# Pooled attention and token/channel mixer on one core: cast DMAs in long rows, pooling by GpSimd adds, shared batch tails and a hand-woven TensorE order

## The chip, the core and the metric

The kernel runs on one core of one Trainium2 chip. The metric is the device time of one execution in microseconds (us). The engines are TensorE (PE; its weight loads are shown as PEld), VectorE (DVE), ScalarE (ACT), GpSimd (POOL) and SyncE (SP); 16 DMA engines move data between the device memory and the on-chip buffer. TensorE writes only into PSUM, eight banks of 2 KB per partition, from which VectorE or ScalarE carries results away.

## The reference

For each of 8 batches: attention of 8 heads with 576 tokens and head size 64, whose keys and values are first averaged over groups of 8 tokens (72 pooled tokens), and then a mixer with a token layer (576 to 256 to 576) and a channel layer (512 to 1536 to 512).

```python
k_p = k.reshape(B, H, 72, 8, 64).mean(axis=3)
v_p = v.reshape(B, H, 72, 8, 64).mean(axis=3)
scores = scale * (q @ k_p.transpose(0, 1, 3, 2))
attn = exp(scores - max) / (sum + 1e-09)
x = (attn @ v_p).transpose(0, 2, 1, 3).reshape(B, 576, 512)
h = relu(x.transpose(0, 2, 1) @ w_tok1) @ w_tok2
u = x + h.transpose(0, 2, 1)
out = u + relu(u @ w_ch1) @ w_ch2
```

## The kernel before

576 tokens are four blocks of 128 and one of 64 (`csize`). All matmuls are in bf16. `load_qkv` copies q, k and v of a batch by 15 DMAs from the GpSimd queue that also convert float32 to bf16; each takes one block of tokens and its rows in the device memory are 64 floats (256 bytes) long. Weights come by SyncE's queue in float32 and are cast by ScalarE and VectorE.

Stage A of a batch pools k and v on TensorE: ten matmuls of 512 columns with the averaging matrix `p_full` (L118, L120). It then transposes the pooled keys (L131) and q (L141), and makes scores per head with a contraction over 64 rows, in a piece of 512 columns and one of 64 (L153, L155); ScalarE takes their exponents (L157, L158). `mk_av` multiplies by the pooled values with a column of ones beside them (L169), so that VectorE can divide by the sum (L173, L175). Stage B is the token layer (L189, L203) with transposes of `u` (L208). Stage C is the channel layer: per block of 128 hidden channels four matmuls of 512 columns and four of 64 (L226, L229), evacuated by ScalarE and VectorE in turn, and then for each of the five token blocks twelve matmuls of 512 columns (L246), whose sum VectorE adds to `u` (L249) and ScalarE's queue writes out.

Five batches are in flight: iteration `it` works on stage A of batch `it`, its `mk_av` steps one iteration later, stage B two, stage C three and four later. `weave` spreads the steps of those lists evenly over each other, and a scheduler then orders the instructions of every engine; 12 iterations run. PSUM has four one-bank buffers `pa`, two of `pb` and two of `pt`.

Of the kernel before, what the change touches and what calls it, by code (L numbers as in the profile page):

```python
# [26 lines left out]
):  # L27
    nc = tc.nc
    B, H, S, D = q.shape
    P = 128  # L30
    NC = 5
    TAIL = S - 4 * P
    POOL = 8
    SP = S // POOL
    DM = H * D
    DT = moe_w_tok1.shape[1]
    DC = moe_w_ch1.shape[1]
    scale = 1.0 / (D ** 0.5)
# [25 lines left out]

    w_tok1_sb = singles.tile([P, NC, DT], BF16)
    w_tok2_sb = singles.tile([P, 2, S], BF16)
    w_ch1_sb = singles.tile([P, 4, DC], BF16)
    w_ch2_sb = singles.tile([P, 12, DM], BF16)

    with tc.tile_pool(name="wtmp", bufs=1) as wtmp:  # L70
        wf1 = wtmp.tile([P, NC, DT], FP32, name="wf")
        nc.sync.dma_start(out=wf1[:, 0:4, :], in_=moe_w_tok1[0:4 * P, :].rearrange("(c p) n -> p c n", p=P))
        nc.sync.dma_start(out=wf1[0:TAIL, 4, :], in_=moe_w_tok1[4 * P:S, :])
        nc.gpsimd.memset(w_tok1_sb[:, 4, :], 0.0)
        nc.vector.tensor_copy(out=w_tok1_sb[:, 0:4, :], in_=wf1[:, 0:4, :])
        nc.vector.tensor_copy(out=w_tok1_sb[0:TAIL, 4, :], in_=wf1[0:TAIL, 4, :])

        wf2 = wtmp.tile([P, 2, S], FP32, name="wf")
        nc.sync.dma_start(out=wf2, in_=moe_w_tok2.rearrange("(c p) n -> p c n", p=P))
        nc.vector.tensor_copy(out=w_tok2_sb, in_=wf2)  # L80

        wf3 = wtmp.tile([P, 4, DC], FP32, name="wf")
        nc.sync.dma_start(out=wf3, in_=moe_w_ch1.rearrange("(c p) n -> p c n", p=P))
        nc.scalar.copy(out=w_ch1_sb[:, 0:2, :], in_=wf3[:, 0:2, :])
        nc.vector.tensor_copy(out=w_ch1_sb[:, 2:4, :], in_=wf3[:, 2:4, :])

        wf4 = wtmp.tile([P, 12, DM], FP32, name="wf")
        nc.sync.dma_start(out=wf4, in_=moe_w_ch2.rearrange("(c p) n -> p c n", p=P))
# [166 lines left out]
    def weave(lists):  # L255
# [83 lines left out]
```

## Time and profile before

| | |
|---|---|
| three runs | 382.47, 383.92 (median) and 386.97 us |
| the profiled execution, first to last instruction (its span) | 382.7 us |
| its end: last matmul group L246 from 365.58 to 378.66 us, last L249 at 378.68 us | some 4 us behind the last matmul |
| TensorE matmuls | 339.0 us busy, 89%, 2320 |
| VectorE, ScalarE, GpSimd | 164.0 (43%), 122.4 (32%), 106.2 us (28%) |
| bytes read from and written to the device memory | 35.78 and 9.44 MB |

The profile lists no separate device time for the execution that it shows; its span lies within the three runs and 1.2 us under their median. Matmuls overlap in the pipeline, so that the duration of one (380 ns for 512 columns) is longer than the distance to the next (some 217 ns), and a busy TensorE is not one at its peak. The pace of TensorE is therefore read from the starts of successive matmuls.

### The profile page before, as it was taken

Reading aid. Unit: us, or ns where it says so; the run is one execution under the profiler, and the core shown is the slowest. Engines: PE = TensorE matmul, PEld = TensorE weight load, DVE = VectorE, ACT = ScalarE, POOL = GpSimd, SP = SyncE. Lnnn points to the kernel's source line nnn. Section 1 sums busy time; section 2 is a strip of 40 time slices with the busy share of each in tenths; the row PEclk is TensorE's granted clock in tenths of the full one; section 3 lists DMA queues with packets and bytes.
Section 4 is the critical chain, followed back from the end, with each engine's and each line's share of the span. In section 5 each row is a group of like instructions: output and inputs, shape, how many; then the busy total and the mean of one; then the engine's idle time right before and its main releaser. Section 6 shows DMA issues by size and latency. Waiting matters only on the chain.

```text
span 382.7 us, 5680 instructions
## 1 busy us (share of the span) xinstructions
PE 339.0 (89%) x2320; PEld 158.9 (42%) x2320; DVE 164.0 (43%) x389; ACT 122.4 (32%) x299; POOL 106.2 (28%) x138
## 2 busy tenths in 40 slices
PE   0305657999999999999999999999999999999995
PEld 0002233445544444444445444444444544444442
DVE  1003025665664455354454554445545544443332
ACT  1005519465633353244323451335312212112100
POOL 9819469889717300813000000000000000000000
PEclk9999999999999999999999999999999999999999
DMA  9999999999939471989000100001100101111122
GB/s 146 211 299 120 314 158 124 148 102 140 118 22 143 56 71 41 82 98 93 27 15 27 57 27 15 27 29 42 29 29 28 57 14 57 38 32 55 55 70 69
DMA packets 120745, 31.43 MB, mean 82 GB/s; under 512 B 113232, under 2 KB 113808, under 8 KB 120720
## 3 DMA queue, kind: packets, MB, share of 16 engines
q0 software_dynamic: 112512, 14.16, 60.4%
q10 hardware_dynamic: 5248, 9.44, 7.2%
q1 hardware_dynamic: 2960, 7.47, 5.6%
q8 instruction: 18, 0.29, 0.3%
q14 instruction: 7, 0.06, 0.1%
HBM read 35.78 MB, written 9.44 MB: 118 GB/s over the span
## 4 chain that ended last, share of the span: by engine, by line
PE 83%; DMA 8%; POOL 5%; ACT 2%; issue 0%; DVE 0%; POOLq 0%
PE pa L246 28%; PE pa L226 23%; PE pa L189 5%; PE pa L203 5%; PE pa L153 4%; DMA qb<-in_q_dram 4%; DMA vb<-in_v_dram 4%; PE pb L169 4%; PE pb L229 3%; PE pt L208 3%; PE pa L118 2%; PE pa L120 2%; PE pt L141 2%; POOL vb L100 2%; POOL qb L100 2%; POOL kb L100 2%
## 5 line engine op out<-in xcount | busy, mean ns | idle before, releaser
L246 PE MATMUL pa<-w_ch_sb,GT 128*128 128x512 bf16 (+1 forms) x480 | 112.3, 380 | 0.0
L226 PE MATMUL pa<-uT,w_ch_sb 128*128 128x512 bf16 x384 | 102.6, 380 | 0.0
L249 DVE TENSOR_TENSOR o<-pa,u 128x512 f32<-128x512 f32 (+1 forms) x40 | 27.6, 690 | 91.6 <-PE pa L246 91.6
L246 PEld LDWEIGHTS <-GT 128*128 128x128 bf16 (+1 forms) x480 | 44.9, 100 | 49.5 <-issue 3.6
L232 ACT ACTIVATE GT<-pa 128x512 bf16<-128x512 f32 x48 | 28.7, 597 | 82.4 <-PE pa L226 57.9
L157 ACT ACTIVATE expT<-pa 72x512 bf16<-72x512 f32 x64 | 37.3, 597 | 37.9 <-PE pb L155 35.2
L226 PEld LDWEIGHTS <-w_ch_sb 128*128 128x128 bf16 x384 | 31.2, 98 | 34.3 <-issue 10.8
L144 ACT COPY qT<-pt 128x512 bf16<-128x512 bf16 (+1 forms) x40 | 21.4, 546 | 74.4 <-PE pt L141 74.3
L100 POOL DMA_DIRECT2D qb<-in_q_dram x40 | 36.1, 912 | 28.9 <-PE pb L229 18.5
L118 PE MATMUL pa<-kb,p_full 128*72 128x512 bf16 (+1 forms) x40 | 18.4, 464 | 27.2 <-DMA kb<-in_k_dram 27.2
L235 DVE TENSOR_SCALAR GT<-pa 128x512 bf16<-128x512 f32 x48 | 33.1, 690 | 21.0 <-PE pa L226 20.5
L100 POOL DMA_DIRECT2D vb<-in_v_dram x40 | 37.4, 936 | 9.2 <-DMA qb<-in_q_dram 9.2
L100 POOL DMA_DIRECT2D kb<-in_k_dram x40 | 35.8, 896 | 6.2 <-PE pa L120 4.3
L175 DVE TENSOR_TENSOR x<-pb,den 128x256 bf16<-128x256 f32 (+1 forms) x80 | 32.8, 420 | 1.7
L205 DVE TENSOR_TENSOR u<-pa,x 128x512 bf16<-128x512 f32 (+1 forms) x40 | 27.2, 679 | 11.1 <-PE pa L203 11.0
L229 PEld LDWEIGHTS <-w_ch_sb 128*128 128x128 bf16 x384 | 23.3, 98 | 20.2 <-DVE x L175 0.6
L229 PE MATMUL pb<-uT,w_ch_sb 128*128 128x64 bf16 x384 | 26.4, 193 | 0.0
L169 PE MATMUL pb<-vp,expT 72*128 72x65 bf16 (+1 forms) x320 | 23.4, 201 | 2.3 <-ACT expT L158 2.2
L153 PE MATMUL pa<-qT,kpT 64*72 64x512 bf16 x64 | 24.3, 451 | 1.2 <-ACT qT L144 0.6
L122 DVE CAST kp<-pa 72x512 bf16<-72x512 f32 x8 | 5.5, 685 | 45.3 <-PE pa L118 45.3
L125 POOL MEMSET vp<- 72x8 bf16 x8 | 1.5, 191 | 83.9 <-issue 42.9
L203 PE MATMUL pa<-AT,w_tok_sb 128*128 128x512 bf16 (+1 forms) x80 | 24.5, 380 | 0.0
(44 smaller groups left out, 261.9 us busy)
## 6 DMA issues: line engine op xcount, KB each, us to landing
out_dram<-o ACTq DMA_DIRECT2D x32, 256.0 KB, 2.0
wf<-in_moe_w_ch_dram SPq DMA_DIRECT2D x2, 3072.0 KB, 14.4
qb<-in_q_dram POOLq DMA_DIRECT2D x32, 128.0 KB, 4.5
kb<-in_k_dram POOLq DMA_DIRECT2D x32, 128.0 KB, 4.9
vb<-in_v_dram POOLq DMA_DIRECT2D x32, 128.0 KB, 5.3
out_dram<-o ACTq DMA_DIRECT2D x8, 128.0 KB, 2.3
wf<-in_moe_w_tok_dram SPq DMA_DIRECT2D x1, 576.0 KB, 6.6
wf<-in_moe_w_tok_dram SPq DMA_DIRECT2D x1, 512.0 KB, 3.5
```

The lines of the kernel that those rows point to most:

```text
L100: nc.gpsimd.dma_start(out=dst[0:cs, c], in_=src_[b, :, c * P:c * P + cs, :].rearrange("h p d -> p h d"))
L153: nc.tensor.matmul(out=sc_ps, lhsT=kpT_sb[hl * D:(hl + 1) * D, pr, :], rhs=qT_sb[hl * D:(hl + 1) * D, pr, 0:512], start=True, stop=True)
L157: nc.scalar.activation(out=expT_sb[:, h, 0:512], in_=sc_ps, func=AF.Exp, scale=scale)
L169: nc.tensor.matmul(out=ao[half][0:cs, hh, :], lhsT=expT_sb[:, h, c * P:c * P + cs], rhs=vp_sb[:, h, :], start=True, stop=True)
L175: nc.vector.tensor_tensor(out=x_sb[0:cs, c, half * 4 * D:(half + 1) * 4 * D].rearrange("p (h d) -> p h d", d=D), in0=ao[half][0:cs, :, 0:D ...
L203: nc.tensor.matmul(out=u_ps[0:cs, :], lhsT=w_tok2_sb[:, m, c * P:c * P + cs], rhs=AT_sb[:, m, :], start=(m == 0), stop=(m == 1))
L226: nc.tensor.matmul(out=g_ps, lhsT=w_ch1_sb[:, kk, m * P:(m + 1) * P], rhs=uT_sb[:, kk, 0:512], start=(kk == 0), stop=(kk == 3))
L229: nc.tensor.matmul(out=g_ps2, lhsT=w_ch1_sb[:, kk, m * P:(m + 1) * P], rhs=uT_sb[:, kk, 512:S], start=(kk == 0), stop=(kk == 3))
L232: nc.scalar.activation(out=GT_sb[:, m, 0:512], in_=g_ps, func=AF.Relu)
L235: nc.vector.tensor_scalar(out=GT_sb[:, m, 0:512], in0=g_ps, scalar1=0.0, scalar2=None, op0=ALU.max)
L246: nc.tensor.matmul(out=o_ps[0:cs, :], lhsT=GT_sb[:, kk, c * P:c * P + cs], rhs=w_ch2_sb[:, kk, :], start=(kk == 0), stop=(kk == 11))
L249: nc.vector.tensor_tensor(out=o_sb[0:cs, :], in0=o_ps[0:cs, :], in1=u_sb[0:cs, c, :], op=ALU.add)
```

## The change

Nearly all of the kernel is written anew; the mathematics and the bf16 matmuls stay.

- Tokens are grouped by p = t // 9 and r = t % 9. With that, one partition reads 9 whole rows of q (2304 bytes), and one partition of k or v reads the 8 tokens of a pooled token (2048 bytes). A batch is loaded by three converting DMAs in place of 15 (batch 0 by six), and the weights by converting DMAs as well, all from the GpSimd queue but `w_tok2`, which comes by SyncE's queue and is cast on chip.
- k and v are pooled by additions (`pool8`): three per half tensor, on VectorE for batch 0, on GpSimd for the others. The pooled keys are written twice, side by side, and their transposes go into a 128-row buffer of which one half is zero, so that scores contract over 128 rows in pieces of 320 and 256 columns.
- The ninth block r (64 tokens) of two batches shares one 128-row tile `xt`; the tails of all eight batches make one more channel-layer unit of 512 tokens (n == B). A unit is then 48 matmuls L287 and 48 matmuls L300 of 512 columns, and there are nine units.
- The orders of TensorE and GpSimd are those of the code (`manual_schedule`); VectorE and ScalarE are still ordered by the scheduler. Unit n carries as its side the attention and token layer of batch n + 1, batch 0's stand alone ahead of unit 0. PSUM: three one-bank `p1`, two two-bank `p2`, one `pt`.

```diff
-    for src_, dst in ((q, qb), (k, kb), (v, vb)):
-        nc.gpsimd.dma_start(out=dst[0:cs, c],
-                            in_=src_[b, :, c * P:c * P + cs, :].rearrange("h p d -> p h d"))
+    def load(b):
...
+        parts = 2 if b == 0 else 1
+        def kv(t, src, g):
+            n = H // parts
+            nc.gpsimd.dma_start(out=t[:, g * n:(g + 1) * n].rearrange("j h i d -> j h (i d)"),
+                                in_=src[b, g * n:(g + 1) * n].rearrange("h (j i) d -> j h (i d)", i=POOL))
+        for g in range(parts):
+            kv(kr, k, g)
+            n = HP // parts
+            nc.gpsimd.dma_start(
+                out=qb[:, g * n * BR * D:(g + 1) * n * BR * D].rearrange("p (a e) -> p a e", a=n),
+                in_=q[b, 2 * g * n:2 * (g + 1) * n].rearrange("(a l) (p r) d -> (l p) a (r d)", l=2, r=BR))
+        for g in range(parts):
+            kv(vr, v, g)
...
+    def load_ch():
+        for g in range(3):
+            cols = slice(g * 512, (g + 1) * 512)
+            nc.gpsimd.dma_start(out=w_ch1[:, :, cols], in_=moe_w_ch1[:, cols].rearrange("(c p) n -> p c n", p=P))
+        for g in range(2):
+            nc.gpsimd.dma_start(out=w_ch2[:, 6 * g:6 * g + 6, :],
+                                in_=moe_w_ch2[g * 768:(g + 1) * 768, :].rearrange("(c p) n -> p c n", p=P))
+    def pool8(eng, t, hs, dst, dup):
+        n = hs.stop - hs.start
+        t4 = att.tile([SP, H // 2, 4, D], FP32, name="t4")
+        eng.tensor_tensor(out=t4[:, 0:n], in0=t[:, hs, 0:4], in1=t[:, hs, 4:8], op=ALU.add)
+        eng.tensor_tensor(out=t4[:, 0:n, 0:2], in0=t4[:, 0:n, 0:2], in1=t4[:, 0:n, 2:4], op=ALU.add)
+        if dup:
+            eng.tensor_tensor(out=dst, in0=t4[:, 0:n, 0, None, :].broadcast_to([SP, n, 2, D]),
+                              in1=t4[:, 0:n, 1, None, :].broadcast_to([SP, n, 2, D]), op=ALU.add)
+        else:
+            eng.tensor_tensor(out=dst, in0=t4[:, 0:n, 0], in1=t4[:, 0:n, 1], op=ALU.add)
...
+            eng = nc.vector if first else nc.gpsimd
...
+        def score(hp, odd):
+            n, c0 = (OD, EV) if odd else (EV, 0)
...
+                    nc.tensor.matmul(out=ps[0:SP, hl, 0:n], lhsT=kT[:, odd, h * SP:(h + 1) * SP],
+                                     rhs=st["qT"][:, hp, hl, 0:n], start=True, stop=True)
...
+                nc.scalar.activation(out=exv[:, 2 * hp:2 * hp + 2, c0:c0 + n], in_=ps[0:SP, :, 0:n],
+                                     func=AF.Exp, scale=scale)
...
+        steps += [av(c) for c in range(5)]
+        steps += [at(0), at(1), u(0), u(1), uT(0), u(2), uT(1), u(3)]
+        steps += ([u(4), uT(2), uT(4)] if par else [uT(2)]) + [uT(3)]
...
+        return [g(m) for m in range(NM)] + [o(c, part) for c in range(4) for part in range(3)]
...
+    with tc.manual_schedule(engines={PE, POOLE}):
+        load(0)
...
+        make_identity(nc, ident)
+        load_tok()
+        load_ch()
+        load(1)
+        batches = [batch_steps(b) for b in range(B)]
+        batches[0][0]()
+        for s in batches[0][1]:
+            s()
+        for n in range(B + 1):
+            main = unit_steps(n, batches[n][2] if n < B else None)
+            side = []
+            if n + 1 < B:
+                load(n + 2)
+                batches[n + 1][0]()
+                side = batches[n + 1][1]
+            lo, hi = (14, 26) if n == 0 else (0, 22)
+            at = [lo + i * (hi - lo) // max(1, len(side)) for i in range(len(side))]
+            for i in range(max(len(main), hi + 1)):
+                if i < len(main):
+                    main[i]()
+                for j, s in enumerate(side):
+                    if at[j] == i:
+                        s()
```

How the orders stand at three places. On TensorE before, in the middle of the program, a score of 64 contraction rows stands between groups of the channel layer and of `mk_av`:

```order
L246 MATMUL pa<-w_ch_sb,GT 128x512
L153 LDWEIGHTS kpT
L153 MATMUL pa<-qT,kpT 72x512
L155 LDWEIGHTS kpT
L155 MATMUL pb<-qT,kpT 72x64
L169 LDWEIGHTS expT
L169 MATMUL pb<-vp,expT 128x65
```

On TensorE now, at the start of unit 1 (`pt_769` takes the pooled keys of batch 2 and `pt_780` the first part of its q; both are the one buffer `pt`; rows that repeat are left out):

```order
L287 MATMUL p1_763<-uT_388,w_ch1_86 128x512
L176 LDWEIGHTS kp_734
L176 MATMUL pt_769<-ident_82,kp_734 128x72
...
L189 LDWEIGHTS qb_358
L189 MATMUL pt_780<-ident_82,qb_358 128x128
...
L287 LDWEIGHTS w_ch1_86
L287 MATMUL p1_787<-uT_388,w_ch1_86 128x512
```

The 64-row shapes are gone from such places; what stands between two uses of `pt` is at some places four channel matmuls, and here, between L176 and L189, nothing.

On GpSimd now, at the start of unit 1 (`kr_727` and its fellows are batch 3; `kr_356` is batch 2, whose keys TensorE wants from unit 1 on):

```order
L85 DMA kr_727<-in_k_dram 72x8x512
L90 DMA qb_729<-in_q_dram 128x4x576
L85 DMA vr_728<-in_v_dram 72x8x512
L153 MEMSET vp_735 72x8
L154 MEMSET ex_736 72x64
L130 TENSOR_TENSOR t4_739<-kr_356 72x1024
L131 TENSOR_TENSOR t4_739<-t4_739 72x4x128
L133 TENSOR_TENSOR kp_734<-t4_739 72x512
```

Before, that queue held only DMA issues and a small memset; now the pooling of a batch stands behind the issue of the next one's load, whose q has to wait until the buffer of the batch two before it has been transposed.

On VectorE now, for batch 0, the transposed keys are copied only behind the pooling of its values:

```order
L133 TENSOR_TENSOR kp<-t_149 72x512
L130 TENSOR_TENSOR t_153<-vr 72x1024
L130 TENSOR_TENSOR t_157<-vr 72x1024
L131 TENSOR_TENSOR t_153<-t_153 72x4x128
L131 TENSOR_TENSOR t_157<-t_157 72x4x128
L136 TENSOR_TENSOR vp<-t_153 72x4x64
L136 TENSOR_TENSOR vp<-t_157 72x4x64
L169 MEMSET xt 128x256 x2
L180 COPY kTs_91<-pt 64x288 x4
```

Before, VectorE's part ahead of the scores was three instructions (L122, L126, L133), with no load of its own to wait for.

## Rows read from the trace of the kernel before

**Rows 1.** The page: busy time, and PE and DMA in 40 slices of the span.
```profile
PE 339.0 (89%) x2320; PEld 158.9 (42%) x2320; DVE 164.0 (43%) x389; ACT 122.4 (32%) x299; POOL 106.2 (28%) x138
PE   0305657999999999999999999999999999999995
DMA  9999999999939471989000100001100101111122
```

**Rows 2.** Chain of waits in time: start, length (us), what.
```profile
10.90 15.74 DMA qb<-in_q_dram
...
38.71 15.09 DMA vb<-in_v_dram
...
85.71 0.97 PE pa L226 x4
...
157.31 1.18 PE pa L189 x5
...
198.48 1.18 PE pa L189 x5
...
239.65 1.18 PE pa L189 x5
...
365.58 13.08 PE pa L246 x60
378.68 0.68 DVE o L249
```

**Rows 3.** Timeline of PE, steady part: start, length (us), line, operation, out<-in, shapes, count.
```profile
202.19 0.39 PE L141 MATMUL pt<-ident,qb 128*128 128x128 bf16 x4
202.41 1.03 PE L226 MATMUL pa<-uT,w_ch_sb 128*128 128x512 bf16 x4
203.28 0.28 PE L229 MATMUL pb<-uT,w_ch_sb 128*128 128x64 bf16 x4
203.39 0.29 PE L169 MATMUL pb<-vp,expT 72*128 72x65 bf16 x4
203.53 0.39 PE L141 MATMUL pt<-ident,qb 128*128 128x128 bf16 x4
...
212.93 0.82 PE L246 MATMUL pa<-w_ch_sb,GT 128*128 128x512 bf16 x3
213.68 0.22 PE L155 MATMUL pb<-qT,kpT 64*72 64x64 bf16 x1
213.83 2.12 PE L246 MATMUL pa<-w_ch_sb,GT 128*128 128x512 bf16 x9
215.88 0.40 PE L153 MATMUL pa<-qT,kpT 64*72 64x512 bf16 x1
216.12 0.19 PE L155 MATMUL pb<-qT,kpT 64*72 64x64 bf16 x1
216.24 1.04 PE L226 MATMUL pa<-uT,w_ch_sb 128*128 128x512 bf16 x4
```

**Rows 4.** Groups by line and shape: busy us, mean ns of one, idle before.
```profile
L205 DVE TENSOR_TENSOR u<-pa,x 128x512 bf16<-128x512 f32 x32 | 21.9, 685 | 10.7 <-PE pa L203 10.6
L175 DVE TENSOR_TENSOR x<-pb,den 128x256 bf16<-128x256 f32 x64 | 26.4, 422 | 1.5
L173 DVE RECIPROCAL den<-pb 128x4 f32<-128x4 f32 x64 | 10.8, 176 | 21.1 <-PE pb L169 21.0
L213 DVE COPY uT<-pt 128x512 bf16<-128x512 bf16 x16 | 6.8, 423 | 7.6 <-PE pt L208 7.6
L133 DVE COPY kpT<-pt 128x288 bf16<-128x288 bf16 x8 | 2.4, 305 | 1.7 <-PE pt L131 1.7
L157 ACT ACTIVATE expT<-pa 72x512 bf16<-72x512 f32 x64 | 37.3, 597 | 37.9 <-PE pb L155 35.2 <-PE pa L153 2.3
```

**Rows 5.** Page: DMA queues, packets, MB, share of 16 engines' span (q0: GpSimd's, q1: SyncE's).
```profile
q0 software_dynamic: 112512, 14.16, 60.4%
q1 hardware_dynamic: 2960, 7.47, 5.6%
```

**Rows 6.** Timeline of all engines, start of the program.
```profile
0.81 0.41 SPq L72 DMA_DIRECT2D wf<-in_moe_w_tok_dram  x1
4.34 0.90 DVE L75 CAST w_tok_sb<-wf 128x1024 bf16<-128x1024 f32 x1 [4.34 <-DMA wf<-in_moe_w_tok_dram]
15.15 0.58 PE L120 MATMUL pa<-vb,p_full 128*72 128x512 bf16 x1 [0.38 <-DMA vb<-in_v_dram]
17.91 0.58 PE L120 MATMUL pa<-vb,p_full 128*72 128x512 bf16 x1 [0.34 <-DMA vb<-in_v_dram]
31.82 0.45 PE L131 MATMUL pt<-ident,kp 72*64 72x72 bf16 x8 [0.23 <-DVE kp L122]
32.54 1.75 DVE L85 CAST w_ch_sb<-wf 128x3072 bf16<-128x3072 f32 x1
32.57 2.21 POOL L100 DMA_DIRECT2D vb<-in_v_dram  x1
43.45 1.49 PE L120 MATMUL pa<-vb,p_full 128*72 128x512 bf16 x3
43.56 0.22 ACT L158 ACTIVATE expT<-pb 72x64 bf16<-72x64 f32 x1 [0.30 <-PE pb L155]
```

**Rows 7.** Groups by line and shape, POOL.
```profile
L100 POOL DMA_DIRECT2D qb<-in_q_dram x40 | 36.1, 912 | 28.9 <-PE pb L229 18.5 <-DMA kb<-in_k_dram 7.9 <-PE pa L153 2.4
L60 POOL TENSOR_SCALAR_AFFINE_SELECT p_full<-p_full 128x360 bf16<-128x360 bf16 x1 | 0.5, 505 | 0.0
L59 POOL MEMSET p_full<- 128x360 bf16 x1 | 0.4, 402 | 0.0
```

More of the change, by code (lines that the diff above doesn't have):

```diff
@@ L12 @@
 ALU = mybir.AluOpType
+PE = mybir.EngineType.PE
+POOLE = mybir.EngineType.Pool
 @with_exitstack
@@ L68 @@
[L68 to L88, printed above, removed]
-        nc.scalar.copy(out=w_ch2_sb[:, 0:6, :], in_=wf4[:, 0:6, :])
-        nc.vector.tensor_copy(out=w_ch2_sb[:, 6:12, :], in_=wf4[:, 6:12, :])
@@ L181, in stage_B @@
-    def stage_B(x_sb, u_sb, uT_sb):
-        AT_sb = moe_pool.tile([P, 2, DM], BF16, name="AT")
-        steps = []
-        def mk_AT(m):
-            def s_AT():
-                at_ps = ps_big.tile([P, DM], FP32, name="pa")
-                for c in range(NC):
-                    cs = csize[c]
-                    nc.tensor.matmul(out=at_ps, lhsT=w_tok1_sb[0:cs, c, m * P:(m + 1) * P], rhs=x_sb[0:cs, c, :],
-                                     start=(c == 0), stop=(c == NC - 1))
+    raw = ctx.enter_context(tc.tile_pool(name="raw", bufs=2))
@@ new lines @@
+    ident = singles.tile([P, P], BF16)
+    w_tok1 = singles.tile([P, 6, DT], BF16)
+    w_tok2 = singles.tile([P, 2, S], BF16)
+    w_tok2t = singles.tile([P, 2, 2, P], BF16)
+    w_ch1 = singles.tile([P, 4, DC], BF16)
+    w_ch2 = singles.tile([P, NM, DM], BF16)
+    f2 = singles.tile([P, 2, S], FP32)
+    uT_tails = singles.tile([P, 4, 4 * P], BF16)
+    u_tails = singles.tile([P, 4, DM], BF16)
+    kTs = [singles.tile([P, 2, H * SP], BF16, name=f"kTs{i}") for i in range(2)]
+    loaded = {}
@@ L215, in stage_B @@
[L215 to L224 removed]
+                    nc.vector.tensor_scalar(out=st["AT"][:, m, :], in0=ps, scalar1=0.0, scalar2=None, op0=ALU.max)
+                tails[b // 2, par] = st["AT"]
@@ new lines, in at, with u, go @@
+            return go
+        def u(c):
+            def go():
+                ps = ps_one.tile([P, 512], FP32, name="p1")
+                if c < 4:
+                    mms = [(w_tok2[:, m, c * P:(c + 1) * P], st["AT"][:, m, :]) for m in range(2)]
+                    dst, x = st["u"][:, c, :], st["x"][:, c, :]
+                else:
+                    mms = [(w_tok2t[:, m, half, :], tails[b // 2, half][:, m, :]) for half in range(2) for m in range(2)]
+                    dst, x = u_tails[:, b // 2, :], st["xt"]
+                for i, (w, a) in enumerate(mms):
+                    nc.tensor.matmul(out=ps, lhsT=w, rhs=a, start=(i == 0), stop=(i == len(mms) - 1))
+                nc.vector.tensor_tensor(out=dst, in0=ps, in1=x, op=ALU.add)
+            return go
@@ new lines, in batch_steps @@
+        if first:
+            steps = [kpT(0, HP), qT(0), score(0, 0), score(0, 1), qT(1), score(1, 0), score(1, 1),
+                     kpT(HP, H), qT(2), score(2, 0), score(2, 1), qT(3), score(3, 0), score(3, 1)]
+        else:
+            steps = [kpT(0, H), qT(0), qT(1)]
+            for hp in range(HP):
+                steps += [score(hp, 0)] + ([qT(hp + 2)] if hp + 2 < HP else []) + [score(hp, 1)]
+        steps += [av(c) for c in range(5)]
+        steps += [at(0), at(1), u(0), u(1), uT(0), u(2), uT(1), u(3)]
```

370 lines of the change are left out of this document (161 added, 209 removed).

## The prediction

> **What bounds the kernel now.** I read the page first: TensorE is busy 89% of the span, VectorE 43%, ScalarE 32%, GpSimd 28%. In the 40 slices of 9.57 us TensorE stands at 9 from the eighth on, while the DMA engines are full only in the first eleven [rows 1]. So there are two stages. In the first the chain of waits runs through loads: two pieces of over 15 us are DMAs of q and v, and the channel layer begins only at 85.71 us [rows 2]. In the second the chain is TensorE almost alone; equal points of successive iterations (L189 x5) stand 41.17 us apart, and behind the last matmul come 4.0 us of addition, store and end [rows 2].
>
> What fills 41.17 us? The timeline of TensorE gives prices by starts. 60 matmuls of 512 columns take 13.08 us, 0.218 each [rows 2]. Four transposes take 0.22, four L229 of 64 columns 0.11, four L169 of 65 columns 0.14 [rows 3]. Before, an iteration of all stages has 10 pooling matmuls, 10 in each half of the token layer, 48 in L226 and 60 in L246 (138 x 0.218 = 30.1), 16 scores (2.0), 48 small L229 (1.3), 40 L169 (1.4), 36 full transposes' worth of q and u and 8 of keys (2.3): 37.1 us. Scores of 64 rows cost more than their columns: the nine L246 from 213.83 should end at 215.79, but L153 starts at 215.88, and L153 with L155 hold TensorE until 216.24 where their columns need 0.25; a lone L155 between L246 takes 0.10 before it and 0.15 itself [rows 3]. That is 0.2 us per change of shape and back, eight to twelve per iteration with the other 64-row pieces: some 2.5. About 1.5 us, 4%, remain unexplained.
>
> **The change, TensorE.** A unit's main part is 96 matmuls of 512 columns: 20.9 us. A side: 10 in the first half of the token layer and 8 in the second (12 where the tail pair is made), on average 20 x 0.218 = 4.4; scores with 8 x (320 + 256) columns, worth nine of 512, 2.0; 40 `av` matmuls 1.4; 38 transposes 2.1; 8 of keys 0.3. Sum 10.1. There are nine main parts and seven sides woven in. Removed are the 80 pooling matmuls (17.4 us) and the 96 L246 of the fifth token blocks (20.9), for which the tail unit has 48 (10.5). The 384 small L229 (10.6 us) cost what the 48 hidden-layer matmuls of the tail unit do. The 64-row shapes go: some 20 us over eight iterations. That alone puts 382.7 near 335.
>
> **New waits on TensorE.** The one buffer `pt` makes each group of transposes wait until the last has been copied out: end of pipeline 0.2 us, then two copies of 576 columns (L133 took 305 ns for 288; I estimate 0.45 each) [rows 4]. Between the keys and the first q nothing stands: 1.1 us in every side. Elsewhere four channel matmuls (0.87 us) cover 0.2 + 0.42 of a copy like L213 [rows 4]. An `av` block costs VectorE a reciprocal and twice the columns of L175, 0.18 + 0.69 [rows 4]; with two `p2` buffers a pair of blocks without filler waits some 0.4. I take 1.5 us per side. A unit with side is then 20.9 + 10.1 + 1.5 = 32.5.
>
> VectorE and ScalarE carry this: per unit VectorE has 15.5 passes of 0.69 [rows 4] over 512 columns (six of the hidden layer, four outputs, four and a half of u, one AT), five `av` blocks at 0.87, some 4.5 copies at 0.42 and two at 0.45, 17.8 us; ScalarE has eight exponents of 512 to 640 columns (0.6 like L157 [rows 4], and up to 0.73 in proportion), four q copies and seven activations, 12.3 us. Both are under 32.5.
>
> **GpSimd.** A batch is pooled by additions over 2 x (1024 + 512 + 512) elements per partition for k and 2 x (1024 + 512 + 256) for v: 7680. No two-input GpSimd operation is in the trace. Its one-input passes took 402 and 505 ns for 360 elements, 1.1 and 1.4 ns each [rows 7]. One read per element is the lower bound; for two inputs I take twice the dearer, 2.8 ns, 21.5 us, with three DMA issues at 0.91 [rows 7] 24 us per batch. That stands beside 32.5 us of TensorE and costs nothing; it begins to decide at (32.5 - 3.2) / 7680 = 3.8 ns.
>
> The Trainium skill speaks against this move: "GPSIMD Engine Reference", section Engine selection, sends element-wise additions to VectorE and calls GpSimd about twice as slow. Its measured 4497 ns for 2048 elements (section Performance versus the Vector engine) would make 16.9 us per batch by an estimate; by the rule and by the rows the sum stays as it is, since the work is off the path.
>
> **Loads and head.** Rows of 256 bytes become rows of about 2 KB. Two bounds for their rate: SyncE's large unconverted packets, 7.47 MB in 5.6% of 16 engines' span, 349 GB/s [rows 5]; and the old converting DMAs, three of 262 KB between the landings at 15.15 and 17.91 us, 285 GB/s [rows 6]. I take the faster, being nearer in packet size, and keep the other for the range. A landing trails its data by 2 us (0.52 MB issued at 0.81 landed at 4.34, 1.5 us of it data) [rows 6]. Batch 0 with `w_tok2` is 4.1 MB: values land at 0.8 + 0.9 + 11.8 + 2 = 15.5 us (18 by the slower rate). VectorE then adds (1.2 + 2 x 0.69 + 2 x 0.42) and, queued behind that, copies the keys: 4 us, 19.5. Keys to last exponent took the old kernel 31.82 to 43.78 for its first batch [rows 6]; with sixteen exponents where there are eight longer ones now, I take 11.5: 31. Five `av` blocks at 0.9: 35.5. TensorE paces at 0.45 per 512 columns here (three in 1.49), the 1.2 GHz level [rows 6], so AT costs 4.5 in which VectorE also works, and u and its transposes alternate with VectorE for four: 44. Unit 0 starts at 44 us.
>
> Unit 0 has its side packed into 12 steps, so transposes and `av` blocks stand next to each other: 20.9 + 10.5 + 7.5 = 39. It needs batch 1's pooled keys 13 steps in, at some 57. Before those keys lie 12.2 MB in the queue: 0.8 + 0.9 + 35 + 2 = 39; added by 51. Six microseconds spare.
>
> **Sum.** 44 + 39 + 6 x 32.5 + 2 x 20.9 + 4.0 = 324; of the 4% that the old iteration leaves unexplained I put half on the seven woven units, 4: a span of **328 us** against 382.7. The median before is 1.2 above its profiled span: 329 predicted.
>
> **Rivals.**
> - *Batch 1 comes late* (0.10). With the slower rate everything at the start slips by 3 and batch 1's keys by 8, 331 to 334. GpSimd can also be held while it issues: its DMA at 32.57 took 2.21 us beside a VectorE cast of 1.75 us, against 0.91 usually [rows 6, 7], and VectorE now adds for some 10 us while GpSimd issues the weight loads. The Trainium skill ("GPSIMD Engine Reference", Specifications) says that VectorE instructions with two SBUF inputs or in a two-port mode contend with GpSimd; that row agrees for a cast. Ten microseconds more in the queue exceed the spare by 4: 332. If the converting packets run at half the old pace (143 GB/s), keys land at 88 and are added by 100, where 74 is needed after a head that is 17 longer: 17 + 26 more, 371. For it: none of those packets is in the trace. Against: longer rows should not be slower per byte than 256-byte ones.
> - *The woven order waits* (0.13): TensorE is held at each of nine transposes groups by 0.65 us in place of two, since VectorE's queue, ordered by another hand, is behind: 5 us more in each of seven units, 363; with half of it 345. For it: one `pt` buffer where there were two. Against: the channel matmuls between, and VectorE at 17.8 of 32.5.
> - *GpSimd becomes the bound* (0.08), the one that can end slower. Above 3.8 ns per element TensorE waits for pooled keys at each unit's start; at 5.0 a batch takes 41.7 us, 9.2 more in six and a half units: 388, slower than before. Half of this case lies there. For it: no row shows a two-input addition, and the broadcast operands are odd. Against: 5.0 is 3.6 times the dearer row.
> - That the sides are not woven at all is excluded: the order on TensorE is written in the code.
>
> **How the numbers follow.** The forecast (chance 0.69) spans 317 to 338: start faster by 3 to slower by 5, waits per side from 0.8 to 2.5, the rest from nothing to 4%. Late batch 1 gives 331 to 371, waits 338 to 363, GpSimd 338 to 388 and beyond. Taking in half of these cases the range is 316 to 350. One per cent, 4 us, is about what a measurement here can tell from no change. Faster by over 1% 0.94, within 0.02, slower 0.04, the last being GpSimd beyond 5 ns.
>
> **What would show it.** After: L287 and L300 at 0.218 us from start to start, and equal points of two successive units 64 to 67 us apart; unit 0 beginning at 42 to 49 us; GpSimd's additions some 17 to 25 us per batch, with idle time before the q issue; no wait of over 0.5 us on TensorE before the first keys' transpose of units 1 to 6; a gap of about 1 us between L176 and L189. Wrong would be: waits for `kp` or for `kr` in unit 0, a GpSimd without idle time, or units of over 36 us.

## The result, and the profile after

The changed kernel takes 335.6 us, the median of 4 runs (334.15 to 337.6), beside 383.32 us for the kernel before (382.47 to 386.97): a ratio of 0.8738, 95% interval 0.8667 to 0.8809. Predicted were 329 us. Its profiled execution has 336.74 us and a span of 335.0, so the comparison below is 335.0 against the predicted span of 328. Some runs of two experiments were disturbed (in a slower state of the chip); the undisturbed ones are 366.17 us for b2_pool1of5 and 370.69 and 372.29 us for b3_longrows, so the medians of these two stand too high.

The page of the changed kernel, to be held against [rows 1]: busy time, TensorE and its granted clock in 40 slices of 8.4 us, and GpSimd.

```profile
PE 287.1 (86%) x1840; PEld 149.9 (45%) x1840; DVE 157.2 (47%) x304; ACT 96.4 (29%) x161; POOL 152.2 (45%) x142
...
PE   0026879788699998999899899989998999999994
...
PEclk9999999797879999999999999999999999999998
...
POOL 7382398089608950994099329999200000000000
```

TensorE has 480 instructions and 51.9 us of busy time less than before, GpSimd 46 us more. Slices of 8 or 9 begin with the fifth instead of the eighth. New are the sevens and the six up to slice 11 and, in slices 8 and 10 to 12, a granted clock below 9.

Where each stage begins, from TensorE's timeline (start, length, what, and the idle time before with what ended it). These are the first matmuls of the channel layer in units 0, 1 and 2, in 6 (the last woven one), 7 and 8 (the tail unit):

```profile
47.20 1.02 PE L287 MATMUL p_390<-uT,w_ch_86 128*128 128x512 bf16 x4 [0.52 <-DVE uT L261]
...
89.61 1.40 PE L287 MATMUL p_763<-uT,w_ch_86 128*128 128x512 bf16 x4 [0.52 <-DVE uT L261]
...
124.33 1.03 PE L287 MATMUL p_1122<-uT,w_ch_86 128*128 128x512 bf16 x4
...
255.10 1.03 PE L287 MATMUL p_2579<-uT,w_ch_86 128*128 128x512 bf16 x4
288.36 1.03 PE L287 MATMUL p_2917<-uT,w_ch_86 128*128 128x512 bf16 x4
...
309.08 1.03 PE L287 MATMUL p_3058<-uT_tails,w_ch_86 128*128 128x512 bf16 x4
```

Head 47.2, unit 0 42.4, unit 1 34.7, units 2 to 6 32.8 on the mean, units 7 and 8 20.7 and 20.9; the last matmul ends at 330.0. Against the sum of the prediction (44 + 39 + 6 x 32.5 + 2 x 20.9 + 4.0 + 4) the head is 3.2 longer, unit 0 3.4, the end 1.0; units 1 to 6 take 198.8 where 199 were put down with the 4 us of unexplained time. By these sums all that is missed lies before 90 us and in the last microseconds; that unit 1 is longer than its fellows does not show in them, because the 4 us of unexplained time cover it.

TensorE's waits from 123 to 291 us (total, times, longest), the stretch in which [rows 3] stood:

```profile
PE pt L189 <- DVE kTs_92 L180: 3.3, 3, 1.1
PE pt L189 <- DVE kTs_91 L180: 2.2, 2, 1.1
PE p_1318 L214 <- DVE x L222: 0.2, 1, 0.2
```

Five such units wait 1.1 us each for the two copies of the keys and 0.2 for an `av` block (the last row stands for five alike).

GpSimd's work for one batch (timeline; idle time before in brackets), which no row before could price:

```profile
101.37 0.78 POOL L90 DMA_DIRECT2D qb<-in_q_dram  x1 [12.34 <-PE pt L189]
...
103.13 2.13 POOL L130 TENSOR_TENSOR t_1100<-kr 72x1024 f32<-72x1024 bf16 x1
...
121.11 0.84 POOL L85 DMA_DIRECT2D kr<-in_k_dram  x1
```

7680 elements from 103.13 to 121.11: 18.0 us, 2.3 ns per element, and 12.3 us idle before the next q issue.

### The profile page after: what moved, and what is told of

The parts are those of the page before. It is cut to its first block, busy times and chain, and to the rows that moved or that the text cites. A ratio compares the mean times of both kernels' runs of the same rounds, so it can differ in the third digit from the quotient of the medians.

```text
span 335.0 us, 4535 instructions
## 1 busy us (share of the span) xinstructions
PE 287.1 (86%) x1840; PEld 149.9 (45%) x1840; DVE 157.2 (47%) x304; ACT 96.4 (29%) x161; POOL 152.2 (45%) x142
## 4 chain that ended last, share of the span: by engine, by line
PE 77%; DVE 14%; DMA 4%; ACT 2%; issue 2%; POOL 1%; DVEq 0%; POOLq 0%
DVE x L222 4%; DMA vr<-in_v_dram 4%; PE pt L189 4%; PE pt L260 3%; DVE GT L292 2%; DVE u L251 1%; ACT ex L204 1%; DVE kTs_92 L180 1%; DVE den L219 1%; DVE kTs_91 L180 1%; PE p_504 L300 1%; PE p_644 L300 1%; ACT qT L191 1%; DVE uT L261 1%; PE p_3181 L300 1%
## 5 line engine op out<-in xcount | busy, mean ns | idle before, releaser
L300 PEld LDWEIGHTS <-GT 128*128 128x128 bf16 x432 | 40.2, 98 | 40.6 <-issue 1.1
L287 PEld LDWEIGHTS <-w_ch_86 128*128 128x128 bf16 x432 | 41.3, 99 | 38.1 <-issue 2.4
L90 POOL DMA_DIRECT2D qb<-in_q_dram x9 | 6.9, 770 | 65.9 <-PE pt L189 42.9
L191 ACT COPY qT<-pt 128x640 bf16<-128x640 bf16 x32 | 22.1, 690 | 36.6 <-PE pt L189 36.6
L189 PE MATMUL pt<-ident,qb 128*128 128x128 bf16 x160 | 16.2, 239 | 15.6 <-DVE kTs_91 L180 10.1
L189 PEld LDWEIGHTS <-qb 128*128 128x128 bf16 x160 | 12.5, 108 | 21.7 <-issue 17.4
L214 PEld LDWEIGHTS <-ex 72*128 72x128 bf16 x320 | 14.5, 102 | 13.3 <-DVE x L222 7.5
L176 PE MATMUL pt<-ident,kp 72*128 72x72 bf16 x64 | 4.1, 211 | 15.2 <-DVE kp L133 15.2
L261 DVE COPY uT<-pt 128x512 bf16<-128x512 bf16 x32 | 13.4, 418 | 5.0 <-PE pt L260 5.0
L260 PE MATMUL pt<-ident,u 128*128 128x128 bf16 x128 | 12.4, 219 | 2.1 <-DVE uT L261 0.7
L231 PEld LDWEIGHTS <-w_tok_83 128*128 128x128 bf16 x80 | 8.5, 107 | 11.5 <-issue 4.1
L201 PEld LDWEIGHTS <-kTs_91 128*72 128x72 bf16 x64 | 8.1, 129 | 8.9 <-issue 4.3
L176 PEld LDWEIGHTS <-kp 72*128 72x128 bf16 x64 | 3.7, 108 | 17.2 <-DVE kp L133 15.2
L201 PEld LDWEIGHTS <-kTs_92 128*72 128x72 bf16 x64 | 7.2, 115 | 5.9 <-issue 1.0
L250 PEld LDWEIGHTS <-w_tok_84 128*128 128x128 bf16 x64 | 6.1, 99 | 7.2 <-issue 1.4
```

The source lines that it names most:

```text
L189: nc.tensor.transpose(out=ps[:, rr].rearrange("m l p -> m (l p)"), in_=st["qb"][:, o:o + P], identity=ident)
L191: nc.scalar.copy(out=st["qT"][:, hp].rearrange("m l (r p) -> m r l p", p=BP), in_=ps)
L201: nc.tensor.matmul(out=ps[0:SP, hl, 0:n], lhsT=kT[:, odd, h * SP:(h + 1) * SP], rhs=st["qT"][:, hp, hl, 0:n], start=True, stop=True)
L214: nc.tensor.matmul(out=ps[:, h // 4, (h % 4) * (D + 1):(h % 4 + 1) * (D + 1)], lhsT=st["ex"][:, h * S + n0:h * S + n0 + P], rhs=st["vp"][: ...
L231: nc.tensor.matmul(out=ps, lhsT=w_tok1[:, c if c < 4 else 4 + par, m * P:(m + 1) * P], rhs=st["x"][:, c, :] if c < 4 else st["xt"], start= ...
L260: nc.tensor.transpose(out=ps[:, kk, :], in_=src[:, kk * P:(kk + 1) * P], identity=ident)
```

## The experiments

**Two parts of the change alone, in the kernel before.** b1_rows128 gives the scores full rows:

```diff
+    kz = [[singles.tile([P, H // 2, SP], BF16, name=f"kz{i}{hl}") ...]]   # other 64 rows zero
-                nc.tensor.matmul(out=sc_ps, lhsT=kpT_sb[hl * D:(hl + 1) * D, pr, :],
-                                 rhs=qT_sb[hl * D:(hl + 1) * D, pr, 0:512], start=True, stop=True)
+                nc.tensor.matmul(out=sc_ps, lhsT=kz[par][hl][:, pr, :],
+                                 rhs=qT_sb[:, pr, 0:512], start=True, stop=True)
...
```

> The kernel before with one part of the change alone: the scores contract over 128 rows, against key buffers whose other 64 rows hold zeros (one more copy per batch on VectorE). Theory of the prediction (each change to a 64-row shape and back costs TensorE some 0.2 us, and before it ran without slack, so what it saves comes off the time): 13 to 19 us less, 364 to 370 us, with the steady period 41.17 down to about 39.3 to 39.8. Rival (those gaps lie beside waits that take their place, or the price is not the shape's): 380 to 386 us, period above 40.8.

372.8 us, ratio 0.9693 (0.9647 to 0.9738): 11 to 12 us less. In its steady part a pair of scores is followed without a gap, where [rows 3] showed L153 and L155 holding TensorE for 0.36 us:

```profile
216.41 0.38 PE L158 MATMUL pa<-qT,kz 128*72 128x512 bf16 x1
216.62 0.19 PE L160 MATMUL pb<-qT,kz 128*72 128x64 bf16 x1
216.65 0.23 PE L174 MATMUL pb<-vp,expT 72*128 72x65 bf16 x2
```

0.24 us from the first start to the third. Equal points of the chain (L194 x5, answering to L189 x5 in [rows 2]):

```profile
152.38 1.18 PE pa L194 x5
...
191.50 1.18 PE pa L194 x5
...
230.60 1.18 PE pa L194 x5
```

The period is 39.1, so 2.06 us per iteration are the price of the scores' 64 rows, slightly more than expected (39.3 to 39.8). The total fell short of 13 to 19 because the start, which waits for loads, gains little: the channel layer begins at 84.6 us instead of 85.6, and what comes after it got shorter by 10. The granted clock is 0.50 in that start from 48 to 68 us, where the profiled execution of the kernel before has 9 in every slice; whether that took anything from the gain is not shown. Six other executions of the kernel before had a mean granted clock of 0.973 and took 383.36 to 384.79 us, within the spread of those near 1.00 (381.94 to 387.84).

b2_pool1of5 leaves only one of five pooling matmuls (`for c in range(1)` in place of `range(NC)`).

> The kernel before with one of the five pooling matmuls of k and one of v per batch; it leaves out four fifths of the averaging sums. Theory (TensorE is the bound, so 8 x 8 matmuls at 0.218 us come off in full): 14 us less, about 369 us, period 41.17 to 39.4. Rival (they filled waits that stay): 380 to 386.

Median 372.8 of four runs (366.17 to 374.38). The theory's 369 lies between these, and no run came near the rival's 380: TensorE's pooling was on the path. Equal points of its profiled execution:

```profile
189.14 1.18 PE pa L189 x5
...
228.33 1.18 PE pa L189 x5
```

They are 39.2 us apart: 1.98 us less per iteration for eight matmuls, where the theory had 1.74. What the whole run gains stays open.

**The loads alone, in the kernel before** (b3_longrows):

```diff
-                                        in_=src_[b, :, c * P:c * P + cs, :].rearrange("h p d -> p h d"))
+                    flat = src_[b].rearrange("h s d -> (h s d)")[c * P * DM:(c * P + cs) * DM]
+                    ... in_=flat.rearrange("(p n) -> p n", n=DM)
```

> The kernel before with its fifteen loads per batch reading whole rows of 2 KB instead of eight pieces of 256 bytes; q, k and v so hold other tokens in other places, the work is the same. Theory (the loads of the start are what the long rows shorten, the steady period of 41.17 us does not hang on them): 5 to 12 us less, 371 to 378 us, the period between 41.0 and 41.3. Rival 1 (the start is bound by the order and the number of the loads, not by their rows): 381 to 386. Rival 2 (more comes of it, because the whole start, 38 us later in the kernel before than in the changed one, is loads): below 360.

Median 375.0 (370.69 to 380.0); by 370.69 and 372.29 us the ratio is 0.9672 (0.9605 to 0.974), some 12.6 us less. The channel layer begins at 72.9 us, 12.7 earlier, and the period is what it was:

```profile
144.81 1.18 PE pa L190 x5
...
185.98 1.18 PE pa L190 x5
```

The period is 41.17, so all of the gain is start; the theory held at its upper end. In the changed kernel the channel layer begins 38.4 us earlier than before (47.2 instead of 85.6). The long rows account for 12.7 of these; what the others are made of was not tried apart.

**Where the head lost 3 us.** In the changed kernel VectorE adds the values of batch 0 as soon as they land and only then copies the keys, which TensorE had transposed long before:

```profile
15.23 0.42 PE L176 MATMUL pt<-ident,kp 72*128 72x72 bf16 x4 [15.23 <-DVE kp L133]
21.66 0.69 PE L189 MATMUL pt<-ident,qb 128*128 128x128 bf16 x5 [6.01 <-DVE kTs_91 L180]
```

```profile
16.25 1.22 DVE L130 TENSOR_TENSOR t_153<-vr 72x1024 f32<-72x1024 bf16 x1 [0.48 <-DMA vr<-in_v_dram]
17.39 1.21 DVE L130 TENSOR_TENSOR t_157<-vr 72x1024 f32<-72x1024 bf16 x1
...
20.49 0.55 DVE L169 MEMSET xt<- 128x256 uint32 x2
20.95 0.56 DVE L180 COPY kTs_91<-pt 64x288 bf16<-64x288 bf16 x2
```

a2_vlate turns the two round:

```diff
+                if first and h0 == 0:
+                    with tc.issue_after(c.ins):     # c: the copy of the first keys
+                        st["values"]()              # the additions of vr, taken out of prepare
```

> The changed kernel with the values of batch 0 added up behind the first copy of its keys on VectorE, instead of ahead of it. Theory (the head was late because the transposes of q waited 6 us for that copy): the first transposes of q at 17 to 18 us instead of 21.7, unit 0 begins 3.5 to 4.5 us earlier, at 43 to 44, and the run takes 331 to 332 us. Rival (the attention of batch 0 then waits for its second keys or its values and nothing is won): 335 to 336.

330.1 us, ratio 0.8572 (0.8539 to 0.8606): 5.5 less than the changed kernel, somewhat more than expected. The first q now follows the keys, and unit 0 begins 5.1 us earlier:

```profile
17.51 0.69 PE L195 MATMUL pt<-ident,qb 128*128 128x128 bf16 x5 [1.30 <-DVE kTs L183]
...
42.09 5.12 PE L293 MATMUL p<-uT,w_ch 128*128 128x512 bf16 x22 [0.52 <-DVE uT L267]
```

**Why units 0 and 1 are long.** Windows of the changed kernel: from:to, length, busy time and instructions of PE, PEld, DVE, ACT, POOL, then granted clock, DMA share, GB/s.

```profile
60.00:64.00 4.00, 1.78 (x21) 1.31 (x20) 1.51 (x3) 0.73 (x2) 0.00 (x0) 0.85 0.96 185
64.00:68.00 4.00, 4.00 (x24) 2.31 (x23) 0.00 (x0) 2.28 (x4) 0.00 (x0) 0.72 0.04 12
...
72.00:76.00 4.00, 2.68 (x39) 1.56 (x37) 3.10 (x9) 0.31 (x1) 3.84 (x4) 1.00 1.09 205
76.00:80.00 4.00, 3.90 (x18) 1.55 (x19) 1.54 (x4) 0.00 (x0) 3.84 (x4) 0.57 0.81 168
...
88.00:92.00 4.00, 2.46 (x20) 1.29 (x17) 1.34 (x5) 0.60 (x1) 1.03 (x2) 0.77 0.46 52
92.00:96.00 4.00, 3.40 (x16) 1.96 (x17) 1.15 (x2) 1.12 (x2) 0.00 (x0) 0.50 0.59 100
```

Three times TensorE stands in waits of the packed side and the granted clock is low behind it. What that does to a step of four matmuls, and the waits ahead of it:

```profile
62.02 0.44 PE L189 MATMUL pt<-ident,qb 128*128 128x128 bf16 x5 [1.44 <-DVE kTs_92 L180]
63.24 0.69 PE L189 MATMUL pt<-ident,qb 128*128 128x128 bf16 x5 [0.78 <-ACT qT L191]
63.72 1.91 PE L300 MATMUL p_504<-w_ch_87,GT 128*128 128x512 bf16 x4
...
66.38 1.03 PE L300 MATMUL p_504<-w_ch_87,GT 128*128 128x512 bf16 x4
...
76.36 1.80 PE L300 MATMUL p_644<-w_ch_87,GT 128*128 128x512 bf16 x4
77.96 1.91 PE L231 MATMUL p_649<-x,w_tok_83 128*128 128x512 bf16 x4
```

1.91 and 1.80 against 1.03 us for four of the same shape: the pace of the 1.2 GHz level and of the 2.4. Spread out (a1_wide0), and spread with nothing left over behind the last step (a6_in):

```diff
-            lo, hi = (14, 26) if n == 0 else (0, 22)
+            lo, hi = (4, 26) if n == 0 else (0, 22)     # a1_wide0
+            lo, hi = (4, 23) if n == 0 else (0, 22)     # a6_in
```

> The changed kernel with the side of unit 0 spread over 22 of its steps instead of 12. Theory (the packed side makes TensorE wait on single buffers, and the granted clock falls to its lower level behind these waits; both go when the side is spread): unit 0 from 42.4 to 36 to 38 us, the slow stretch in unit 1 gone as well, 328 to 331 us against 335.6. Rival 1 (the keys of batch 1 then come late, or the waits only move): 334 to 338. Rival 2 (waits go, the fall of the clock stays, because it is due to something else): 332 to 334, with granted clock below 0.9 still in three or more windows of 4 us between 47 and 100 us.

329.5 us, ratio 0.856 (0.8521 to 0.8598). Unit 0 lasts 35.4 instead of 42.4, but unit 1 still 34.7: the last pieces of the side stand alone between 78 and 81.75, where unit 1 begins, and in the 4 us behind them the granted clock is 0.51:

```profile
78.00:82.00 4.00, 2.08 (x17) 1.26 (x17) 2.84 (x6) 0.00 (x0) 1.50 (x2) 1.00 0.46 61
82.00:86.00 4.00, 2.76 (x18) 1.70 (x18) 0.91 (x2) 0.96 (x2) 0.00 (x0) 0.51 0.85 151
```

So the half of the theory on unit 0 held; the half on unit 1 did not. Rival 2 had named three windows below 0.9 as its sign, and there are three (0.76, 0.50 and 0.89 in the windows of 4 us from 80 to 92), but its time of 332 to 334 was not met. One of the six runs differs from the others: its mean granted clock is 0.998 and it took 325.87 us, where the other five have 0.985 to 0.990 and 328.88 to 330.23. The same order of instructions thus ran with the fall and without it, and they are 3.0 to 4.4 us apart. The next one takes the leftover pieces away:

> The changed kernel with the side of unit 0 between its steps 4 and 22, so that none of its pieces is left over behind the channel layer's last step (in a1_wide0 the last three were, TensorE was busy 2.1 of 4 us there and the granted clock then 0.51 for 4 us in unit 1). Theory (the clock falls behind stretches in which TensorE waits): no window below 0.9 after 46 us, unit 1 33.3 us instead of 34.7, unit 0 34.5 to 36: 327 to 329 us. Rival (the fall comes at about the same place whatever stands there): unit 1 stays 34.7, 329 to 331.

326.0 us, ratio 0.8476 (0.8441 to 0.851), one below the 327 to 329 expected; all six runs lie within 0.4 us of each other, with a granted clock of 0.999 or 1.000. Unit 0 is 34.8 and unit 1 32.1, the length of the other units of its kind (the 33.3 that I had written is that of the kind with a tail pair). The slice row has no fall left:

```profile
PEclk9999999999999999999999999999999999999999
```

The rival, a fall at the same place whatever stands there, is out. The one run of a1_wide0 without a fall was as fast as a6_in, so what a6_in gains on the others seems to be the fall alone.

**Is GpSimd far from being the bound?** a3_keys_twice adds the keys twice, a4_all_twice all of it (`for _ in range(1 if first else 2):` ahead of the additions).

> The changed kernel with the keys of batches 1 to 7 added up twice on GpSimd (the same sums again). Theory (GpSimd's work lies beside TensorE's and decides only when a batch takes longer than a unit of 32.1 to 33.3 us): a batch goes from 20 to 29.5 us with its issues, which still fits: 334 to 337 us, with GpSimd's idle time before the q issue down from about 12 to about 2 us. Rival (the pooled keys are already the last thing that a unit waits for, or GpSimd's traffic slows VectorE beside it): each of seven units some 3 to 9 us longer, 355 to 395 us.

333.5 us (332.35 to 336.38), ratio 0.868 (0.8618 to 0.8742): no dearer, with the idle time before the q issue down to 2.83 us.

```profile
164.08 0.78 POOL L90 DMA_DIRECT2D qb<-in_q_dram  x1 [2.83 <-PE pt L190]
```

> The changed kernel with keys and values of batches 1 to 7 added up twice on GpSimd. Theory (beyond a unit's length GpSimd becomes the bound): a batch takes 2 x 17.5 + 2.8 = 37.8 us, more than a unit; unit 1 begins at about 96 us instead of 89.6 and the following five each come 37.8 us apart, so the end is 30 to 34 us later: 366 to 370 us, with TensorE waiting for pooled keys or values in each unit. Rival (GpSimd has more room than that, because batches are made ahead): 335 to 345 us. Rival 2 (GpSimd beside VectorE gets slower per element when it is busy throughout): above 375.

374.1 us, ratio 0.9725 (0.9676 to 0.9774), 38.5 above the changed kernel. TensorE now waits for pooled values and keys (waits from 90 to 330 us):

```profile
PE p L216 <- POOL vp L136: 15.2, 6, 3.2
...
PE pt L178 <- POOL kp L133: 5.8, 3, 2.7
```

A batch takes GpSimd 38.5 us, 0.7 more than I put down; over the six units from 94.3 to 325.2 us that makes the 4 us by which the estimate was short. An addition of 1024 elements takes 2.1 us as before, so rival 2 (slower per element) is out. The granted clock also falls behind the waits (0.945 over the run, 0.976 in the changed kernel); that it costs time here is not shown. The two experiments bracket the point of decision. Additions that last 27.5 us per batch (132.90 to 160.42 in a3_keys_twice), 3.6 ns per element of the changed kernel's 7680, cost nothing; 35.9 us (154.89 to 190.80 in a4_all_twice), 4.7 ns, cost 38 us.

**The 1.1 us behind the keys' transposes.** a5_gap sets a step of the channel layer between them and the first q, by one empty piece in the side's list:

```diff
-            steps = [kpT(0, H), qT(0), qT(1)]
+            steps = [kpT(0, H), lambda: None, qT(0), qT(1)]
...
+            for j in range(1, len(side)):
+                at[j] = max(at[j], at[0] + 1) if j >= 2 else at[0]
```

> The changed kernel with one step of the channel layer set between the keys' transposes and the first transposes of q in the seven woven units. Theory (each unit loses 1.1 us there, waiting for two copies out of the one transposition buffer, and a step of 0.87 us covers most of it): 0.9 us less per unit, 6 us in all, 329 to 330 against 335.6. Rival (the wait only moves to the next group of transposes or to the exponents): 334 to 337.

331.0 us, ratio 0.8599 (0.8559 to 0.8639), one above the 329 to 330 expected, and not for the reason given. Units 2 to 6 are only 0.14 us shorter. The empty piece moved all that comes after it, and the second half of the token layer came to stand directly behind the first (waits from 120 to 290 us):

```profile
PE p L250 <- DVE AT L236: 2.8, 5, 0.6
PE pt L189 <- DVE kTs L180: 1.2, 5, 0.2
```

0.9 us of waiting for keys became 0.56 of waiting for `AT` and other small ones. Most of the 4.6 us came from unit 0 (40.6 instead of 42.4) and unit 1 (33.2 instead of 34.7). c3_gap, below, does it without moving the rest.

**The head's pace.** In the changed kernel's head four matmuls of 512 columns take the time of the lower level, although the granted clock of that stretch reads 1.00 (0 to 46 us):

```profile
37.01 1.90 PE L231 MATMUL p_302<-x,w_tok_83 128*128 128x512 bf16 x4
```

```diff
+            steps = [warm(14), kpT(0, HP), warm(12), qT(0), warm(2), score(0, 0), ...   # a7_warm, on a6_in
+                nc.tensor.matmul(out=ps, lhsT=ident, rhs=wz, start=True, stop=True)     # wz: zeros
```

> a6_in with idle matmuls of 512 columns, whose results nobody reads, in the head: 14 before the first keys' transposes, 12 behind them, two in each wait for a copy of q, one behind each av block. Theory (the head's matmuls of 512 columns stand 0.43 us apart, the pace of the lower level, because TensorE waits so much before them; kept busy it goes at 0.22 and the transposes, scores, av blocks and the token layer of batch 0 get shorter): unit 0 begins 3 to 5 us earlier, at 42 to 44 instead of 46.7, and the run takes 321 to 323 us against 326.0. Rival (the pace of the head comes of something else, or the idle matmuls stand in the way): 326 to 330.

324.3 us (323.21 to 327.2), ratio 0.8454 (0.8412 to 0.8496), beside 0.8476 for a6_in: between the two expectations, and within the intervals no difference. Unit 0 begins 2.5 us earlier, at 44.2; 1.4 of it is lost again in unit 0, which now waits 1.2 us for the keys of batch 1. The pace of the first idle matmuls changes while they run: the first four, from 6.54 us, take 1.89 us (0.44 between starts), the last six, from 9.64 us, 1.46 (0.22), and the granted clock reads 1.00 all that time:

```profile
6.54 4.55 PE L178 MATMUL p<-wz,ident 128*128 128x512 bf16 x14 [6.54 <-POOL ident masks.py:199]
```

But behind them the granted clock falls, in 16 to 20 us to 0.57:

```profile
16.00:20.00 4.00, 3.87 (x11) 1.16 (x8) 4.00 (x6) 0.00 (x0) 3.84 (x6) 0.57 0.77 101
```

It is low again in later windows of the head (0.70 from 24 to 28 us, 0.65 from 32 to 36). So the head's matmuls can go at the faster pace when TensorE is kept busy ahead of them, but the granted clock then falls in the head, and how much that took back is not shown. What decides between the two stays open.

**Put together.** c1_even takes the later values of a2_vlate, loads the keys of batch 1 ahead of the channel weights and spreads the side of unit 0 like all the others:

```diff
+        load_k(1)
         load_ch()
...
-            lo, hi = (14, 26) if n == 0 else (0, 22)
+            lo, hi = 0, 22
```

> The changed kernel with the values of batch 0 added behind the first copy of its keys (a2_vlate), the keys of batch 1 loaded ahead of the channel weights, and the side of unit 0 spread over its 22 steps like all the others. Theory (the head loses 4.6 us, unit 0 needs no packing because its keys are there, and the clock does not fall because TensorE does not wait): unit 0 begins at 42 to 43 and lasts 33.3 to 34, units 1 to 6 196.1, and the run takes 319 to 321 us. Rival 1 (the channel weights now come late, 3 us behind the keys): 322 to 326. Rival 2 (the gains do not add, because the granted clock falls elsewhere): 324 to 330.

320.4 us (319.72 to 321.25), ratio 0.8351 (0.8316 to 0.8385). Unit 0 begins at 41.9 and lasts 33.3, units 1 to 6 take 196.1. These came within 0.1 us of what was written, and the special case for unit 0 is gone. The three parts were not tried in this combination one by one; whether the earlier load of the keys was needed is not shown. Last, the step behind the keys with nothing else moved (c3_gap):

```diff
+            for j in (1, 2):
+                at[j:j + 1] = [max(at[j], j)] if side else []
```

> c1_even with the first and second transposes of q one step later in each of the seven woven units, so that a step of the channel layer (0.87 us) stands between the keys' transposes and them, and nothing else moves (in a5_gap every later piece of the side moved too, and the second half of the token layer came to stand directly behind its first, a wait of 0.56 us per unit). Theory (the 1.1 us for two copies out of the one transposition buffer is a loss that filler covers): 0.25 us of it stays per unit, units 31.2 and 32.4 to 32.5 us, 6 us less in all, 314 to 316 us against 320.4. Rival (a wait covered here comes back elsewhere in the unit, as in a5_gap, because something else paces it): units 31.9 to 32.1 and 33.1 to 33.3, 319 to 321.

318.0 us (317.68 to 318.51), ratio 0.8284 (0.8244 to 0.8325): the best here, 17.6 below the changed kernel. It lies between the 314 to 316 of the theory and the 319 to 321 of the rival. In units 1 to 6 theory and rival are each right in half: those with 28 pieces went from 32.1 to 31.2, those with 30 only from 33.3 to 33.2, since in these the third q now stands close behind the second and waits for its copy (waits from 107 to 290 us):

```profile
PE pt L203 <- ACT qT L205: 1.9, 3, 0.6
PE pt L203 <- DVE kTs L191: 1.2, 5, 0.2
```

Unit 0 became 0.45 us longer (33.8): it has the same wait of 0.6 us for a copy of q, and 0.4 for its pooled values.

## Why the prediction came out as it did

- *TensorE as the bound, and the woven unit* (32.5 predicted): right. Two units are 65.4 us apart, 12 matmuls take 2.59 to 2.60, units 1 to 6 sum to 198.8 for 199. That the sum is met so closely is luck in part: 2.6 us of it are the slow stretch in unit 1. Without it the six take 196.1 (c1_even), so that of the 4 us put down for unexplained time some 1.1 were needed. The old period of 41.17 fell to 32.7. Of the 8.5 us, b1_rows128 shows 2.06 for the scores' rows; pooling, the fifth token block and the small L229 are 10 x 0.218 + 12 x 0.218 + 1.3 = 6.1 by [rows 2, 3]. Of these only the pooling was tried (b2_pool1of5, 1.98 for eight matmuls); the shared tails were not tried alone. The 64-row price was put at 2.5. The total of 20 us for the 64-row shapes was too high as a gain on the whole run: it was counted for eight iterations, and b1_rows128, which changes the scores' rows alone, gained 1 us in the load-bound start and 10 behind it.
- *Waits on the single `pt`*: right, 1.11 us between keys and first q, 0.2 for `av` (0.4 predicted). The copies of 576 columns took 454 ns on the mean (estimate 0.45).
- *GpSimd hidden*: right, and shown by a3_keys_twice and a4_all_twice, with the point of decision (3.8 ns) between 3.6 and 4.7. The price was 2.3 ns per element for 2.8. The Trainium skill's rule against the move ("GPSIMD Engine Reference", Engine selection: about twice as slow as VectorE) agrees in size with this trace: 2.13 us on GpSimd and 1.22 on VectorE for the same 1024 elements, 1.75 times. It had no say in the time, because GpSimd's part lies beside TensorE's. The 16.9 us estimated from the Trainium skill's figure ("GPSIMD Engine Reference", Performance versus the Vector engine) is nearer to the measured 18.0 than my 21.5.
- *Head* (44): the mechanism right, the size short by 3.2. The values landed at 16.25 (15.5 predicted), VectorE then took 5.3 us to the end of the keys' copies instead of 4: I priced one addition of 1024 where there are two, and left out the clearing of `xt` (0.55). The attention took 0.6 more, the `av` blocks 1.2 less, and u with its transposes 5.7 instead of 4.
- *Unit 0* (39): this term failed in its size, 42.4, and unit 1 was 2.6 longer than others of its kind. The waits of the packed side were counted (7.5 us; TensorE's waits in unit 0 come to some 7), the fall of the granted clock behind them was not: the clock was taken as full from unit 0 on, as [rows 1] have TensorE at 9 throughout from the eighth slice. a6_in has the same pieces spread, with fewer waits and no fall: 34.8 and 32.1, 10 us less in the two. How these 10 us divide can be estimated from the changed kernel's rows. From 63.24 to 66.38 us TensorE does what takes it 1.7 us right behind, and from 76.36 to 79.99 what takes 1.9: 3.1 us of unit 0 are the clock, nearly all by which it exceeds 39. Unit 1 has the same waits as unit 3 (1.1 and 0.2 us), so its 2.6 are the clock too. That leaves some 4.5 us of the 10 for the waits.
- *The end* (4.0): 5.0. The last result leaves in two issues of SyncE, one behind the other, which take 1.11 us together (from 330.72); before, one issue of 0.47 us did (at 379.40). That is 0.6 of the 1.0 us. It is read from the traces and was not tried; the other 0.4 stays open.
- *Batch 1 late*: not so. Its keys were added up at 48.60 us (51 forecast), and unit 0 asked for them at 60.15, without a wait. GpSimd was not held in its issues either: the five for the channel weights, beside VectorE's additions, took 0.76 and 0.85 us each. So the packing, meant to wait for these keys, bought nothing: a6_in asks for them at 51.04 and does not wait. c1_even, whose unit 0 begins at 41.9, loads them earlier.

The forecast was thus right in its mechanism, but for the granted clock in units 0 and 1, which it did not foresee, and 2% low in its size; the range held it.

## What to carry to other kernels

In this kernel a side packed into few steps of a woven loop cost twice: in its waits, and in the granted clock of what followed them. See first when what the side needs is really there, and spread the side over all steps; loading it earlier was tried here only together with the rest. Before an operation that becomes ready early is set on an in-order queue, look at what stands behind it: six adds that nobody needed for 13 us held the first scores of the program for 4. And when a wait is covered by moving one piece, move that piece alone.

## What the runs showed of the hardware

- The granted clock is low behind some waits but not behind all. In c1_even TensorE is busy 2.05 of 4 us around the start of unit 0 and the clock stays at 1.00:

```profile
40.00:44.00 4.00, 2.05 (x20) 1.24 (x19) 2.14 (x6) 0.60 (x1) 0.00 (x0) 1.00 1.37 185
```

  What decides it was not settled here, and the order of instructions alone does not: one run of a1_wide0 in six had no fall. Nor was it settled why the head's matmuls keep 0.43 us at a granted clock of 1.00, nor why the clock falls in a7_warm's head, where TensorE has more to do.
- GpSimd's additions did not slow VectorE, whose work beside them mostly reads PSUM. With 152.2, 216.5 and 273.2 us of GpSimd work VectorE's busy time is 157.2, 157.2 and 158.3, and its copies of `uT` take 418 ns in the changed kernel and 417 in a4_all_twice.
- GpSimd's DMA issues took longer beside some of VectorE's work. In the kernel before, the issues beside VectorE's two large casts of weights took 2.21 [rows 6] and 1.93 us (at 59.15), the others some 0.9; one beside a cast on ScalarE alone took 0.88 (at 34.76). Beside VectorE's additions of two on-chip inputs in the changed kernel's head nothing of the kind shows: an issue for `w_tok` takes 0.60 us at 12.40, beside an addition, as at 6.34, where VectorE is idle. The Trainium skill ("GPSIMD Engine Reference", Specifications) names instructions with two SBUF inputs and those in a two-port mode as contending with GpSimd; the traces agree for the cast, and for these additions they do not.
